# A one-token attention and ReGLU layer: the query product moves from TensorE to VectorE and GpSimd, x is loaded once, and the down products are placed on a block boundary

## The chip, the cores and the metric

The kernel runs on one core of a Trainium2 chip. A core has five engines that run side by side: PE (TensorE, matmuls), DVE (VectorE), ACT (ScalarE), POOL (GpSimd) and SP (SyncE, which here only issues DMA transfers), and 16 DMA engines that move data between the chip's main memory and the core's SBUF. SBUF and PSUM (where matmuls write) both have 128 partitions. The metric is device time in microseconds (us); lower is better. A change of under 0.2% can't be told from none here.

## The reference

One token passes through a pre-norm attention block with a cache of 8192 positions, and then through a gated feed-forward block. All is float32: D = 640, H = 32 heads of Dh = 192, F = 1536.

```python
def _A_ref(x, k_cache, v_cache, wq, wo):
    q = (x @ wq).reshape(B, Sq, H, Dh).transpose(0, 2, 1, 3)
    scores = jnp.einsum("bhqd,bhkd->bhqk", q, k_cache) * (Dh ** -0.5)
    p = _softmax(scores, axis=-1)
    o = jnp.einsum("bhqk,bhkd->bhqd", p, v_cache)
    return o.transpose(0, 2, 1, 3).reshape(B, Sq, H * Dh) @ wo

def _B_ref(x, W_gate, W_up, W_down):
    gate, up = x @ W_gate, x @ W_up
    return (gate * (gate > 0) * up) @ W_down

h = x + _A_ref(_layernorm(x), k_cache, v_cache, wq, wo)
h2 = h + _B_ref(_layernorm(h), W_gate, W_up, W_down)
```

K and V of one head are 6.29 MB each, so the 64 of them make up 403 of the 446 MB that the kernel reads.

## The kernel before, in words

The kernel writes one list of instructions for each engine with the small class `Eng`: `op(fn, after)` appends an instruction and turns each handle in `after` into a semaphore wait, unless that engine has already waited for that value. Each engine runs its list in order. What is written first in the code is first on its engine, and nothing is scheduled afterwards.

There are three large SBUF buffers: `kt[0]` and `kt[1]` (12288 floats in each partition, one head of K each) and `vt` (one head of V). All large transfers are issued by SP, in order, on one DMA queue (q1 in the profile). Each waits only until its buffer is free. At the start the same three buffers hold the query weights `wq`: `wq_t[0]` and `wq_t[1]` lie in `kt[0]`, 2 and 3 in `kt[1]`, and 4 in the first half of `vt`. A row `wq_t[j]` has 6144 floats, the outputs of all heads, for the inputs p*5 + j of the partitions p. So K of head 0 can be loaded when rows 0 and 1 have been used (`h_kfree[0]`), K of head 1 after rows 2 and 3 (`h_kfree[1]`), and V of head 0 after row 4.

Before the loop over heads: x is loaded twice by ACT's queue (`xT`, 128 partitions x 5 floats, and `xrow`, one row of 640). The layer norm makes `xn`, 128 x 5 (PE sums over partitions, by a product with `ones`). PE then forms q with 60 matmuls (L208) in three PSUM banks, ACT copies it out in 12 pieces into `qd` (L216; four partitions hold a quarter of the heads each, all other entries are zero), and PE broadcasts the 192 values of one head to all partitions with the matrix `sel` (L220, and `next_q` at L230 in the loop).

For each head: DVE multiplies K by q (L290, four pieces), POOL folds the halves together (L292), DVE sums the rest (L296) and takes the maximum, and then `kt[h % 2]` is free and SP issues K of head h+2. ACT takes the exponentials (L309), PE multiplies them with V (L240, 32 matmuls), and then `vt` is free and SP issues V of the next head. PE runs its part as a hardware loop (`Fori`). The last entry of `pe.ops.append(("loop", H, body, 32))` is the place, in a block of 256 instructions, where the loop's first instruction is put. The other engines' lists are unrolled.

Behind the loop come the output projection (L342), the layer norm of h, and the up, gate (L379) and down (L393) products, each waiting for its weights, which come on the same queue into buffers as these are freed.

## Time and profile before

| | |
|---|---|
| median of 3 runs | 1041.15 us (1040.79, 1041.15, 1042.88) |
| the profiled execution's own time | 1042.81 us |
| its span, first to last instruction | 1041.2 us |
| busy share of the span | DVE 64%, POOL 43%, PE 35%, PEld 13%, ACT 5% |
| read from main memory | 445.91 MB, 428 GB/s over the span |
| instructions | 6847 |

The profile is of one execution. Its span leaves out 1.6 us of that execution's time. A line of the profile names the engine, the source line, the tile written and the tiles read ("kt<-kt,bank"), how often, and how long; what stands behind `<-` in square brackets is what ended the engine's idle time. "SPq" and "ACTq" are the moments at which SP and ACT issue a DMA. PEclk, or the granted clock, is the share of TensorE's full clock that it was given. A "DMA share" of 1 means that all 16 DMA engines were at work; values a little above 1 come from how packets are split over the windows.

### The profile page before, as it was taken

The numbers are of one execution on the slowest core, as the hardware profiler recorded it, in microseconds if no ns is written. First come the engines' busy times: TensorE is split into PE (matmuls) and PEld (weight loads), VectorE is DVE, ScalarE is ACT, GpSimd is POOL, SyncE is SP. The second block draws the span as 40 slices with busy tenths as digits, with TensorE's granted clock in tenths as the row PEclk, the third lists the DMA queues.
The fourth block names the chain that finished last, engine by engine and source line by source line (L and its number), as shares of the span: only waits on it lengthen the run. The fifth ranks groups of instructions, "written<-read, shape, count | busy, mean of one in ns | idle before, by whom it ended". The sixth has DMA issues, their size and how long they took to land. (4 is left out here: it accounts for less than half of the span.)

```text
span 1041.2 us, 6847 instructions
## 1 busy us (share of the span) xinstructions
PE 361.2 (35%) x2848; PEld 130.8 (13%) x2848; DVE 670.2 (64%) x400; ACT 47.2 (5%) x150; POOL 442.6 (43%) x135
## 2 busy tenths in 40 slices
PE   1504333322333333222233333322133333322385
PEld 0101110111111111001111111101011111101123
DVE  1079677776666667776666667777666666777001
ACT  0201000000000000000000000000000000000010
POOL 2055555554444455555444445555444445555000
PEclk9856665656666666656666666666666666665698
DMA  9999999999999999999999999999999999999997
GB/s 393 446 427 425 444 429 427 444 429 425 446 427 427 442 431 427 440 432 425 442 432 425 442 432 425 442 432 425 442 429 429 442 429 429 440 429 437 420 427 302
DMA packets 11397, 446.05 MB, mean 428 GB/s; under 512 B 1397, under 2 KB 1401, under 8 KB 2042
## 3 DMA queue, kind: packets, MB, share of 16 engines
q1 hardware_dynamic: 11240, 445.91, 99.3%
q8 instruction: 5, 0.08, 0.0%
q14 instruction: 6, 0.05, 0.0%
q10 hardware_dynamic: 146, 0.01, 0.0%
HBM read 445.91 MB, written 0.00 MB: 428 GB/s over the span
## 5 line engine op out<-in xcount | busy, mean ns | idle before, releaser
L292 POOL TENSOR_TENSOR kt<-kt 128x1536 f32<-128x1536 f32 x128 | 436.6, 3443 | 517.5 <-DVE kt L290 517.5
L290 DVE TENSOR_TENSOR kt<-kt,bank 128x3072 f32<-128x3072 f32 x128 | 420.7, 3349 | 143.1 <-DMA kt<-in_A_k_cache_dram 142.6
L240 PE MATMUL bank<-vt,pr 128*2 128x384 f32 x2048 | 238.7, 635 | 546.4 <-PEq L61 546.4
L296 DVE TENSOR_REDUCE sc<-kt 128x16 f32<-128x1536 f32 x128 | 215.2, 1743 | 0.0
L240 PEld LDWEIGHTS bank<-vt,pr 128*2 128x2 f32 x2048 | 57.9, 101 | 706.9 <-issue 706.9
L302 DVE SCALAR_TENSOR_TENSOR oall<-bank,ind,oall 128x193 f32<-128x193 f32 x32 | 13.4, 420 | 137.9 <-PE bank L244 137.9
L311 ACT COPY ob<-bank 128x384 f32<-128x384 f32 x32 | 15.3, 478 | 806.3 <-PE bank L240 806.3
L244 PE MATMUL bank<-ob,par 128*128 128x192 f32 x128 | 28.4, 345 | 22.4 <-PEq L61 22.4
L244 PEld LDWEIGHTS bank<-ob,par 128*128 128x128 f32 x128 | 19.9, 189 | 44.5 <-issue 44.5
L234 PE MATMUL bank<-rs,ones 128*128 128x1 f32 x64 | 14.2, 291 | 27.7 <-PEq L61 27.7
L217 DVE MEMSET bank<- 128x384 f32 x1 | 0.4, 378 | 28.3 <-ACT zt L216 28.3
L227 PE MATMUL bank<-ident,mp 128*1 128x128 f32 x32 | 8.9, 279 | 26.4 <-PEq L61 26.4
L230 PE MATMUL bank<-zt,sel 128*128 x64 | 18.0, 364 | 0.0
L234 PEld LDWEIGHTS bank<-rs,ones 128*128 128x128 f32 x64 | 12.4, 242 | 29.5 <-issue 29.5
L233 PE MATMUL bank<-m,ones 1*128 1x1 f32 x64 | 11.6, 248 | 9.3 <-PEq L61 9.3
L208 PE MATMUL bank<-kt,xn 128*32 128x512 f32 x96 | 13.4, 717 | 4.1 <-DMA kt<-in_A_wq_dram 2.3
L342 PE MATMUL bank<-kt,oT 128*3 128x480 f32 x96 | 11.5, 644 | 1.6 <-DVE oT L333 1.6
L233 PEld LDWEIGHTS bank<-m,ones 1*128 1x128 f32 x64 | 9.8, 190 | 18.2 <-issue 18.2
L367 DVE STREAM_TRANSPOSE hT<-h 128x160 f32<-128x160 f32 x1 | 0.5, 465 | 17.8 <-ACT h L365 17.8
L309 ACT ACTIVATE pr<-sc,nb 128x64 f32<-128x64 f32 x32 | 11.1, 347 | 1.0
L179 DVE TENSOR_REDUCE s<-xT 128x1 f32<-128x5 f32 x1 | 0.2, 158 | 17.0 <-DMA xT<-in_A_x_dram 17.0
L230 PEld LDWEIGHTS bank<-zt,sel 128*128 128x128 f32 x64 | 9.9, 195 | 3.2
(88 smaller groups left out, 104.0 us busy)
## 6 DMA issues: line engine op xcount, KB each, us to landing
kt<-in_A_k_cache_dram SPq DMA_DIRECT2D x32, 6144.0 KB, 35.4
vt<-in_A_v_cache_dram SPq DMA_DIRECT2D x32, 6144.0 KB, 21.6
kt<-in_A_wq_dram SPq DMA_DIRECT2D x2, 6144.0 KB, 24.9
kt<-in_A_wo_dram SPq DMA_DIRECT2D x2, 5760.0 KB, 34.2
vt<-in_A_wo_dram SPq DMA_DIRECT2D x1, 3840.0 KB, 15.5
zt<-in_B_W_up_dram SPq DMA_DIRECT2D x1, 3840.0 KB, 24.3
vt<-in_A_wq_dram SPq DMA_DIRECT2D x1, 3072.0 KB, 40.3
kt<-in_B_W_gate_dram SPq DMA_DIRECT2D x1, 3072.0 KB, 21.6
```

The lines of the kernel that those rows point to most:

```text
L208: a = pe.op(lambda e, j=j, b=b, g=g, c0=c0: e.matmul(qps[b][g * Q:(g + 1) * Q, :], xn[:, j:j + 1].to_broadcast([P, Q]), wq_t[j][:, c0:c0 + ...
L230: return e.matmul(qb, sel, qd[:, bass.ds(i * DH + DH, DH)], start=True, stop=True)
L233: pe.op(lambda e: e.matmul(pb[:, 0:1], ones[0:1, :], m1, start=True, stop=True), takes=[(to_pe["m1"], 1)], sig=pe.sem)
L234: pe.op(lambda e: e.matmul(po2[:, DH:DH + 1], ones, rs, start=True, stop=True), takes=[(to_pe["exp"], 1)])
L240: pe.op(lambda e, i=i, g=g: e.matmul(po[g * Q:g * Q + 2, :], pr[:, 2 * i:2 * i + 2], vt[:, 2 * i * DH:2 * (i + 1) * DH], start=(i < NQ), s ...
L244: pe.op(lambda e, k=k: e.matmul(po2[:, 0:DH], par[:, k, :], ob[:, k * DH:(k + 1) * DH], start=(k == 0), stop=(k == 1)), takes=[(to_pe["ob" ...
L290: a = dve.op(lambda e, ks=ks, h=h: e.tensor_mul(ks, ks, qb[:, None, :].to_broadcast([P, SUB, DH])), [h_k[h], h_qb[h]])
L292: fold.append(pool.op(lambda e, ks=ks: e.tensor_add(ks[:, :, 0:HD], ks[:, :, 0:HD], ks[:, :, HD:DH]), [a]))
L296: a = dve.op(lambda e, ks=ks, i=i, h=h: e.reduce_sum(sc[h % 2][:, i * SUB:(i + 1) * SUB], ks[:, :, 0:HD], axis=AX.X), [fold[i]])
L302: return dve.op(lambda e: e.scalar_tensor_tensor(oall, po2, ind[:, h:h + 1], oall, op0=ALU.mult, op1=ALU.add), [in_loop(h, T_O), (dve.sem, ...
L311: act.op(lambda e: e.copy(ob, po), [in_loop(h, T_V)], sig=to_pe["ob"])
L342: a = pe.op(lambda e, i=i, j=j, g=g: e.matmul(acc3[g * Q:g * Q + 3, :], oT[:, j:j + 3], wo_t[i][:, j - WJ[i]:j - WJ[i] + 3, g * DG:(g + 1) ...
```

## The change

Four things are changed.

1. The query product. `wq_t[j]` is no longer multiplied on PE. DVE takes its first 5120 columns (`QS`) and POOL the other 1024: each multiplies the row by the per-partition scalar `xn[:, j]` and adds it up in `qd`, which now holds a partial sum in every partition. DVE does multiply and add in one instruction (L211), POOL in two (L213, in place in the weights' buffer, and L214). The sum over partitions is left to the product that broadcast the head's q: it uses `ones` where it used `sel` (L219, L229). The 60 matmuls, the 12 copies of ACT and `sel` are gone. `h_q[j]` is now a pair of handles, one of DVE and one of POOL, and the loads of K and V into `kt` and `vt` wait for both.
2. x is loaded once, as a row. `xT` becomes a PSUM tile that PE writes with five transposes of one column each (L178).
3. POOL zeroes only the last 192 columns of `qd`, which `next_q` reads in the last turn of the loop.
4. The loop's head is put at place 88 of its block instead of 32, and `addr_align` in front of the down products makes them start at the beginning of a block of 256 instructions.

```diff
-    hx = load(xT, x[0, 0].rearrange("(p j) -> p j", p=P), "xT", eng=act)
     hxr = load(xrow, x[0], "xrow", eng=act)
...
-    h_qd = pool.op(lambda e: e.memset(qd, 0.0))
+    h_qd = pool.op(lambda e: e.memset(qd[:, H * DH:], 0.0))
...
-    a = dve.op(lambda e: e.reduce_sum(s1, xT, axis=AX.X), [hx])
+    xT, xj = pa[:, 0:DJ], xrow.rearrange("o (p j) -> o j p", j=DJ)
+    for j in range(DJ):
+        a = pe.op(lambda e, j=j: e.transpose(xT[:, j:j + 1], xj[:, j, :], ident[0:1, 0:1]), [hxr, h_id])
+    a = dve.op(lambda e: e.reduce_sum(s1, xT, axis=AX.X), [a])
...
+    QS = 5 * H * DH // 6
     h_q = []
+    d = q = None
     for j in range(DJ):
-        for b in range(NQB):
-            for g in range(NQ):
-                c0 = g * QW + b * QB
-                a = pe.op(lambda e, j=j, b=b, g=g, c0=c0: e.matmul(
-                    qps[b][g * Q:(g + 1) * Q, :], xn[:, j:j + 1].to_broadcast([P, Q]), wq_t[j][:, c0:c0 + QB],
-                    start=(j == 0), stop=(j == DJ - 1)), [h_xn, hwq[j]])
-        h_q.append(a)
-    h_qc = []
...
-    h_po = dve.op(lambda e: e.memset(po, 0.0), [h_qc[-1]])
+        w, x1 = wq_t[j], xn[:, j:j + 1]
+        wd, wp, ad, ap = w[:, 0:QS], w[:, QS:], qd[:, 0:QS], qd[:, QS:H * DH]
+        if j == 0:
+            d = dve.op(lambda e, wd=wd, x1=x1, ad=ad: e.tensor_scalar(ad, wd, x1, None, op0=ALU.mult), [h_xn, hwq[j]])
+            q = pool.op(lambda e, wp=wp, x1=x1, ap=ap: e.tensor_scalar(ap, wp, x1, None, op0=ALU.mult), [h_xn, hwq[j]])
+        else:
+            d = dve.op(lambda e, wd=wd, x1=x1, ad=ad: e.scalar_tensor_tensor(ad, wd, x1, ad, op0=ALU.mult, op1=ALU.add),
+                       [hwq[j], d])
+            t = pool.op(lambda e, wp=wp, x1=x1: e.tensor_scalar(wp, wp, x1, None, op0=ALU.mult), [hwq[j]])
+            q = pool.op(lambda e, wp=wp, ap=ap: e.tensor_add(ap, ap, wp), [t, q])
+        h_q.append([d, q])
+    h_po = dve.op(lambda e: e.memset(po, 0.0))
...
-    h_qb[0] = pe.op(lambda e: e.matmul(qb, sel, qd[:, 0:DH], start=True, stop=True), [h_seln, h_qc[-1]])
+    h_qb[0] = pe.op(lambda e: e.matmul(qb, ones, qd[:, 0:DH], start=True, stop=True), [h_ones] + h_q[-1] + [h_qd])
...
-    pe.ops.append(("loop", H, body, 32))
+    pe.ops.append(("loop", H, body, 88))
...
+    align = lambda e: e.addr_align(256, offset=0, max_nops=0)
+    pe.op(align, sig=False)
     for j in range(FJ):
```

What this does to the order on the engines, at the places that matter. On DVE, between the layer norm and the first product with K, as a piece of the difference (`zt` is the tile in which `qd` lies, `kt` and `vt` hold the weights `wq`):

```order
 L196 COPY fix<-ident 128x128 x3
-L198 TENSOR_REDUCE sel<-ident 128x1
-L199 COPY sel<-sel 128x127
-L200 TENSOR_REDUCE ind<-ident 128x32
-L201 TENSOR_REDUCE ind<-ident 128x4
-L217 MEMSET bank 128x384
+L198 TENSOR_REDUCE ind<-ident 128x32
+L199 TENSOR_REDUCE ind<-ident 128x4
+L208 TENSOR_SCALAR zt<-kt,xn 128x5120
+L211 SCALAR_TENSOR_TENSOR zt<-kt,xn,zt 128x5120 x3
+L211 SCALAR_TENSOR_TENSOR zt<-vt,xn,zt 128x5120
+L216 MEMSET bank 128x384
```

Five instructions of 5120 columns now stand ahead of the first product with K (L290). On POOL, the list of after at the same place, with the semaphores that each waits for:

```order
L163 MEMSET zt 128x192
L209 TENSOR_SCALAR zt<-kt0,xn 128x1024 [waits dma_k0,s_dve]
L213 TENSOR_SCALAR kt0<-kt0,xn 128x1024
L214 TENSOR_TENSOR zt<-zt,kt0 128x1024 [waits s_pool]
L213 TENSOR_SCALAR kt1<-kt1,xn 128x1024 [waits dma_k1]
L214 TENSOR_TENSOR zt<-zt,kt1 128x1024 [waits s_pool]
L213 TENSOR_SCALAR kt1<-kt1,xn 128x1024
L214 TENSOR_TENSOR zt<-zt,kt1 128x1024 [waits s_pool]
L213 TENSOR_SCALAR vt<-vt,xn 128x1024 [waits dma_w4]
L214 TENSOR_TENSOR zt<-zt,vt 128x1024 [waits s_pool]
```

Nine instructions stand where POOL had none; all of them read SBUF while DVE's read SBUF too. On SP, the first rows of before:

```order
L142 DMA kt<-in_A_wq_dram 128x12288
L142 DMA vt<-in_A_wq_dram 128x6144
L142 DMA kt<-in_A_k_cache_dram 128x12288 [waits s_pe] x2
L142 DMA vt<-in_A_v_cache_dram 128x12288 [waits s_pe]
L142 DMA kt<-in_A_k_cache_dram 128x12288 [waits s_dve]
```

and of after:

```order
L140 DMA kt<-in_A_wq_dram 128x12288
L140 DMA vt<-in_A_wq_dram 128x6144
L140 DMA kt<-in_A_k_cache_dram 128x12288 [waits s_pool,s_dve] x2
L140 DMA vt<-in_A_v_cache_dram 128x12288 [waits s_pool,s_dve]
L140 DMA kt<-in_A_k_cache_dram 128x12288 [waits s_dve]
```

The transfers stand in the same order; the first three of the cache wait for POOL and DVE now, where they waited for PE.

## The prediction

> **What bounds the kernel now.** I read the page's slices, the queues and what SP waits for first, then the start and the end in order of time.

> ```profile
> DMA  9999999999999999999999999999999999999997
> DMA packets 11397, 446.05 MB, mean 428 GB/s; under 512 B 1397, under 2 KB 1401, under 8 KB 2042
> q1 hardware_dynamic: 11240, 445.91, 99.3%
> q8 instruction: 5, 0.08, 0.0%
> ...
> q10 hardware_dynamic: 146, 0.01, 0.0%
> ...
> SPq L142 <- PE bank L240: 887.7, 32, 29.3
> SPq L142 <- PE bank L208: 43.8, 3, 28.9
> ...
> kt<-in_A_k_cache_dram SPq DMA_DIRECT2D x32, 6144.0 KB, 35.4
> vt<-in_A_v_cache_dram SPq DMA_DIRECT2D x32, 6144.0 KB, 21.6
> kt<-in_A_wq_dram SPq DMA_DIRECT2D x2, 6144.0 KB, 24.9
> vt<-in_A_wq_dram SPq DMA_DIRECT2D x1, 3072.0 KB, 40.3
> xT<-in_A_x_dram ACTq DMA_DIRECT2D x1, 2.5 KB, 18.0
> ```

> The DMA engines are full in every slice but the last. One transfer of 6.29 MB takes 6.29 / 0.428 = 14.7 us, yet K lands 35.4 us after its issue and V 21.6 us: they stand in the queue for 21 and 7 us. SP's long waits for PE therefore cost nothing as long as an issue comes before the queue runs dry. So the time is: start of the stream + bytes / rate + what follows the last bytes. The change leaves the bytes alone (445.91 MB, less 2.5 KB). It can only move the first three issues of K and V, and the end.

> The start, in order of time:

> ```profile
> 0.74 0.87 SPq L142 DMA_DIRECT2D kt<-in_A_wq_dram  x2
> 18.75 0.16 DVE L179 TENSOR_REDUCE s<-xT 128x1 f32<-128x5 f32 x1 [16.98 <-DMA xT<-in_A_x_dram]
> 22.52 0.23 DVE L188 TENSOR_SCALAR xn<-xc,rstd 128x5 f32<-128x5 f32 x1
> 22.80 8.03 PE L208 MATMUL bank<-kt,xn 128*32 128x512 f32 x48 [1.75 <-DVE par L191]
> 24.24 0.37 DVE L201 TENSOR_REDUCE ind<-ident 128x4 f32<-128x128 f32 x1
> 30.98 7.97 SPq L142 DMA_DIRECT2D kt<-in_A_k_cache_dram  x2
> 33.14 5.36 PE L208 MATMUL bank<-kt,xn 128*32 128x512 f32 x48 [2.30 <-DMA kt<-in_A_wq_dram]
> ...
> 38.63 0.33 SPq L142 DMA_DIRECT2D kt<-in_A_k_cache_dram  x1
> 41.98 4.41 PE L208 MATMUL bank<-vt,xn 128*32 128x512 f32 x24 [3.49 <-DMA vt<-in_A_wq_dram]
> 46.54 0.33 SPq L142 DMA_DIRECT2D vt<-in_A_v_cache_dram  x1
> 52.92 0.98 PE L220 MATMUL bank<-zt,sel 128*128 128x192 f32 x2 [6.53 <-ACT zt L216]
> 56.50 13.15 DVE L290 TENSOR_TENSOR kt<-kt,bank 128x3072 f32<-128x3072 f32 x4 [3.19 <-DMA kt<-in_A_k_cache_dram]
> ...
> 0.00:2.00 2.00, 0.00 (x0) 0.00 (x0) 0.84 (x4) 0.24 (x1) 1.40 (x7) 1.00 0.75 221
> 2.00:4.00 2.00, 0.00 (x0) 0.00 (x0) 0.00 (x0) 1.04 (x1) 2.00 (x1) 1.00 0.56 172
> ```

> The weights land at about 18.6 us (the mean of two is 24.9, and the second came 31.9 after its issue at 1.2), 33.1 and 42.0. K of head 0 was issued at 30.98, K of head 1 at 38.63, V at 46.54, and q was ready at 53.9, still 2.6 us before K landed at 56.50.

> **When the queue runs dry.** In the first 4 us 0.79 MB moved, which at 428 GB/s is 1.8 us of work. From an issue into an empty queue (0.74) the stream thus loses 4.0 - 0.74 - 1.8 = 1.4 us. Query weights (15.73 MB) and K of head 0 (6.29 MB) take 51.4 us from an effective start at 2.2, to 53.6. An issue of K of head 1 up to 53.6 - 1.4 = 52.2 us costs nothing. Each us later is lost for good, since nothing behind it has spare time on a full queue. The limits of the others are softer: K of head 0 by 2.2 + 15.73 / 0.428 - 1.4 = 37.5, V 14.7 us after K of head 1's limit.

> **The change, part by part.**

> ```profile
> L292 POOL TENSOR_TENSOR kt<-kt 128x1536 f32<-128x1536 f32 x128 | 436.6, 3443 | 517.5 <-DVE kt L290 517.5
> L290 DVE TENSOR_TENSOR kt<-kt,bank 128x3072 f32<-128x3072 f32 x128 | 420.7, 3349 | 143.1 <-DMA kt<-in_A_k_cache_dram 142.6
> L166 POOL MEMSET zt<- 128x6336 f32 x1 | 5.4, 5377 | 0.0
> ...
> L292 POOL TENSOR_TENSOR kt<-kt x128: 3428/3440/3474, 59.9 to 957.3; 128x1536 f32<-128x1536 f32 x128
> L290 DVE TENSOR_TENSOR kt<-kt,bank x128: 3344/3348/3356, 56.5 to 953.4; 128x3072 f32<-128x3072 f32 x128
> ...
> 62.00:64.00 2.00, 0.00 (x0) 0.00 (x0) 2.00 (x2) 0.00 (x0) 2.00 (x2) 0.50 0.91 393
> ```

> 1. *x as one row.* `xT` was 128 pieces of 20 bytes, 8 for each DMA engine, taking turns with weight rows of 48 KB at 428/16 = 26.8 GB/s, 1.84 us each: 8 turns and one for the semaphore make 16.6 us, about the 18.0 shown. One row has one piece: two turns, so I take it to land near 7 us. The lower bound is about 2, the upper 22 (the old 18.0 and two turns more). Five transposes can't cost more than five times L220's 0.98 us; I take 1.5, since they are of one column and not of 192. The norm takes 4.0 us as before (18.75 to 22.75) and the small DVE work behind it 1.9 (22.7 to 24.6). DVE is ready at 7 + 1.5 + 4.0 + 1.9 = 14.4, before the weights at 18.6. With both upper bounds it is ready at 32.8, and K of head 0 is issued at 44.0, 6.5 us after its limit; I give that no chance of its own, because two turns would have to last like eleven. The stream itself gains the 128 small packets: 146 packets of q10 show 0.0%, so 0.1 us at most.

> 2. *DVE's share.* By L290's 1.09 ns per column, 5120 columns take 5.6 us, 28 us in all. Rows 0 and 1: 18.6 to 29.8, so K of head 0 is issued at 29.8, against 30.98. Rows 2 and 3: 33.1 to 44.3, and K of head 1 is issued at 44.3, against 38.63: later, but 7.9 us before the limit. Row 4: to 49.9, and V at 49.9, against 46.54, inside its limit.

> 3. *POOL's share.* The addition by L292's 2.24 ns per column: 2.3 us for 1024. The scaling has one input and is bounded by L166's 0.85 (0.9 us) and L292's 2.24 (2.3 us); I take 1.0, near the memset. That is 1.0 for row 0 and 3.3 for each other, less than DVE's 5.6, so it is hidden behind DVE if both run side by side, as L290 and L292 do in the window of 62 to 64 us.

> 4. *q and the first head.* PE forms q after 49.9, about 1.0 us (L220), and no copy of ACT follows: 50.9 against 53.9. K lands at 56.5 either way, so the earlier q gains nothing and DVE has 5.6 us of cover. PE has no work in which the 60 matmuls' absence could show.

> 5. *Removed:* 60 matmuls, 12 copies, `sel`: all beside the stream, nothing. The shorter memset: nothing, since POOL is idle there until 18.6.

> 6. *The end.* The weights of the down product land last:

> ```profile
> 1026.02 3.43 PE L379 MATMUL bank<-kt,hT 128*32 128x384 f32 x40 [2.52 <-DMA kt<-in_B_W_gate_dram]
> 1032.62 6.37 PE L393 MATMUL bank<-kt,guT 128*32 128x160 f32 x96 [3.17 <-DMA kt<-in_B_W_down_dram]
> ...
> 1028.00:1030.00 2.00, 1.45 (x20) 0.37 (x12) 0.41 (x1) 0.00 (x0) 0.00 (x0) 1.00 0.96 407
> 1032.00:1034.00 2.00, 1.38 (x24) 1.20 (x28) 0.00 (x0) 0.00 (x0) 0.00 (x0) 0.50 0.86 337
> 1034.00:1036.00 2.00, 2.00 (x36) 1.70 (x32) 0.00 (x0) 0.00 (x0) 0.00 (x0) 0.50 0.23 92
> 1036.00:1038.00 2.00, 2.00 (x39) 1.66 (x35) 0.00 (x0) 0.00 (x0) 0.00 (x0) 0.50 0.05 17
> ...
> 1032.48 0.14 issue
> 1032.62 6.49 PE bank L393 x96
> ```

> L393 runs without a gap from the landing of its first weights: 96 records in 6.49 us. A start on a block boundary can take no stall away, for there is none. What holds it is the clock of 0.50. L379 does 40 records of 384 columns in 3.43 us at 1.00, so 96 of 160 columns would take 3.43 x (96 x 160) / (40 x 384) = 3.4 us; then the last bytes (about 1037) would bound, and the end would come some 2 us sooner. That is the distance of the runs, 1040.79 and 1042.88, and the profiled execution (1042.81) is of the slower sort. I read it as the phase of the clock's changes, which the edit doesn't touch. Skipping to the boundary costs at most a fetch of instructions. PE is through L379 at 1029.45 and its next weights come at 1032.48, so 3 us of it are covered.

> [...]

> **Sum.** Against the profiled execution's own 1042.8: -0.1 for the small packets, 0 for all else, 1042.7 with the slow clock at the end and about 1040.9 with the other. The median of the runs, 1041.15, is of the second sort. I forecast 1041.2.

> **The rivals.**

> *DVE and POOL shut each other out (slower).* L290 has one input in SBUF and one in PSUM, and L296 one in all. They overlap with POOL freely. The new DVE instructions have two SBUF inputs (`kt`, `zt`), and no row shows such a one beside POOL, so it may be that they take turns, an instruction at a time. The bounds: free (44.3 as above), or wholly in turn. In turn, rows 2 to 4 begin at 33.1. Before K of head 1 stand DVE's rows 2, 3 and, because row 4 has landed at 42.0 and each engine slips in when the other ends, row 4 too: 3 x 5.6 + 2 x 3.3 = 23.4, so the issue comes at 56.5. That is 4.3 us past 52.2: about 1045.4. With the scaling at 2.3 us it would be 6.9 us, 1048.1. If POOL were let through before DVE's row 4, it would be 17.8 us, issue at 50.9, and nothing lost. It decides from 52.2 us on. For it: the cover is only 7.9 us and the turns would need 12.2. Against it: nothing in this trace shows such a turn. The two engines' other pairs cost each other nothing: L290 varies from 3344 to 3356 ns, its first run without POOL included, and L292 from 3428 to 3474.

> [...]

> *The end is lifted (faster).* In the windows from 1034 to 1038 a share of 0.23 and 0.05 of the DMA engines is still at work: a few engines finish some 3 us behind the others. If these lag because of code that PE fetched during the stream, then 60 fewer matmuls take some of it away: up to 3 us, 1038. Against it: queue q8, which carries code, shows 5 packets and 0.08 MB in all, and which engine lags for what I can't tell.

> *The jump stalls PE (slower).* A fetch of over 3 us in the full queue would show at the end: 1042 to 1043.

> **How the numbers follow.** Forecast 0.50; turns of DVE and POOL 0.38; lifted end 0.08; jump 0.04. The forecast alone is 1040.6 to 1042.9. With the turns' 1045.4, and 1046.2 for part of the dearer scaling, the range is 1039.8 to 1046.2; it leaves out most of the lifted end and the turns' upper bound. A measurement of this kernel can't tell 0.2% (2.1 us) from no change: below 1039.07 is faster, above 1043.23 slower. Faster 0.08, same 0.52 (the forecast and half of the jump), slower 0.40.

> **What would show it.** Right: x lands near 7 us; DVE's L208 and L211 take 5.6 us and POOL's L213/L214 1.0 and 2.3 while both run; K of head 1 is issued near 44 us, the DMA share shows no hole between 52 and 60 us; L290 starts at 56.5. Wrong: L211 or L214 stretched to the length of the other engine's instruction, SP waiting for POOL until 56 us, a hole of some 4 us in the DMA share, and all that follows later by it.

## The result: 1046.78 us, 0.54% slower, and the profile after

The changed kernel takes 1046.78 us (median of 5 runs, 1046.48 to 1047.96), beside 1041.15 for the kernel before (by now five runs, 1040.79 to 1042.88). The ratio is 1.0054, 95% interval 1.004 to 1.0069. The profiled execution took 1046.48 us, with a span of 1045.0. The forecast of 1041.2 and its range up to 1046.2 were wrong. What happened is the rival "DVE and POOL shut each other out", with a larger price than it was given.

First the start of the changed kernel in order of time. The columns are start, length, engine and line, tiles, how many; in brackets stands the idle time before. L208 and L211 are DVE's share of the five rows, L209, L213 and L214 are POOL's.

```profile
2.06 0.73 PE L178 MATMUL bank<-ident,xrow 1*128 1x1 f32 x5 [2.06 <-DMA xrow<-in_A_x_dram]
18.55 2.89 DVE L208 TENSOR_SCALAR zt<-kt,xn 128x5120 f32<-128x5120 f32 x1 [10.19 <-DMA kt<-in_A_wq_dram]
18.70 5.44 POOL L209 TENSOR_SCALAR zt<-kt,xn 128x1024 f32<-128x1024 f32 x1 [17.21 <-DMA kt<-in_A_wq_dram]
32.98 25.03 SPq L140 DMA_DIRECT2D kt<-in_A_k_cache_dram  x2
33.05 11.87 DVE L211 SCALAR_TENSOR_TENSOR zt<-kt,xn,zt 128x5120 f32<-128x5120 f32 x2 [5.30 <-DMA kt<-in_A_wq_dram]
33.12 8.20 POOL L213 TENSOR_SCALAR kt<-kt,xn 128x1024 f32<-128x1024 f32 x1 [0.24 <-DMA kt<-in_A_wq_dram]
41.40 5.73 POOL L214 TENSOR_TENSOR zt<-zt,kt 128x1024 f32<-128x1024 f32 x1
45.03 7.44 DVE L211 SCALAR_TENSOR_TENSOR zt<-vt,xn,zt 128x5120 f32<-128x5120 f32 x1
47.11 8.07 POOL L213 TENSOR_SCALAR kt<-kt,xn 128x1024 f32<-128x1024 f32 x1
55.27 2.34 POOL L214 TENSOR_TENSOR zt<-zt,kt 128x1024 f32<-128x1024 f32 x1
57.58 2.84 POOL L213 TENSOR_SCALAR vt<-vt,xn 128x1024 f32<-128x1024 f32 x1
```

The same four DVE instructions one by one, in the view of source line L211 (least, median and longest in ns, then the first and last start):

```profile
L211 DVE SCALAR_TENSOR_TENSOR zt<-kt,xn,zt x3: 5552/6284/6286, 21.5 to 38.6; 128x5120 f32<-128x5120 f32 x3
L211 DVE SCALAR_TENSOR_TENSOR zt<-vt,xn,zt x1: 7441/7441/7441, 45.0 to 45.0; 128x5120 f32<-128x5120 f32 x1
```

Read POOL first. Alone, from 55.27 on, its addition takes 2.34 us and its scaling 2.84. Beside DVE they take 5.73, and 8.20 and 8.07. Now see where the long ones end. DVE's row 2 runs from 33.05 for 5.55 us, to 38.60, and row 3 for 6.29 us, to 44.92. POOL's scaling, begun at 33.12, ends at 41.32, which is 2.7 us after row 2. The addition, begun at 41.40, ends at 47.13, 2.2 us after row 3. The scaling begun at 47.11 ends at 55.18, 2.7 us after row 4. Each POOL instruction got next to nothing done until the DVE instruction beside it was over, and then took its own length.

DVE is held too, but by less. Row 2, first to start, takes 5.55 us. Row 3 takes 6.29, 0.73 more; beside it begins POOL's scaling, which has one tile as input. Row 4 takes 7.44, 1.89 more, beside an addition of two tiles. So in the chain from 33.05 to the issue of K of head 1, the terms are three DVE instructions of 5.55 (16.7), 0.73 and 1.89 by which DVE was held, then the rest of the scaling (2.7) and the addition (2.34), and some 0.3 of small gaps. They add up to 24.6 us. The two issues that L140 lists from 32.98 span 25.03 us; the second came 0.33 before their end, at 57.68.

What SP waited for, in the waits of its queue (us in total, times, longest), and the shares in windows of 4 us (PE, PEld, DVE, ACT and POOL busy, then granted clock, DMA share, GB/s):

```profile
SPq L63 <- POOL zt L214: 60.0, 3, 30.8
```

```profile
52.00:56.00 4.00, 0.00 (x0) 0.00 (x0) 0.85 (x2) 0.00 (x0) 3.92 (x2) 1.00 0.09 37
56.00:60.00 4.00, 0.00 (x0) 0.00 (x0) 0.00 (x0) 0.00 (x0) 4.00 (x2) 1.00 0.66 197
60.00:64.00 4.00, 0.98 (x2) 0.50 (x2) 0.00 (x0) 0.00 (x0) 2.76 (x2) 1.00 0.86 369
```

The three issues that the change moves all waited for POOL's L214. From 52 to 56 us the DMA engines stand at a share of 0.09; DVE is done by 52.9 and only POOL is at work. That hole is the loss, and nothing makes it up behind it. In the page's slices it is the one digit that differs from before, and at the end the down product starts later:

```profile
DMA  9989999999999999999999999999999999999997
```

```profile
1037.64 5.24 PE bank L395 x96
```

This line is from the chain that ended last. In the profile before, an execution of 1042.81 us, the down product began at 1032.62; here it is 5.0 us later.

### The profile page after: what moved, and what is told of

It reads as the page before. It is cut to its first block, busy times and chain, and to the rows that moved or that the text cites. A ratio compares the mean times of both kernels' runs of the same rounds, so it can differ in the third digit from the quotient of the medians.

```text
span 1045.0 us, 6621 instructions
## 1 busy us (share of the span) xinstructions
PE 342.9 (33%) x2733; PEld 127.0 (12%) x2733; DVE 698.4 (67%) x403; ACT 41.0 (4%) x138; POOL 481.0 (46%) x144
## 3 DMA queue, kind: packets, MB, share of 16 engines
q1 hardware_dynamic: 11240, 445.91, 99.0%
HBM read 445.91 MB, written 0.00 MB: 427 GB/s over the span
## 5 line engine op out<-in xcount | busy, mean ns | idle before, releaser
L292 POOL TENSOR_TENSOR kt<-kt 128x1536 f32<-128x1536 f32 x128 | 436.5, 3444 | 466.9 <-DVE kt L290 466.9
L290 DVE TENSOR_TENSOR kt<-kt,bank 128x3072 f32<-128x3072 f32 x128 | 420.7, 3349 | 149.3 <-DMA kt<-in_A_k_cache_dram 137.0
L296 DVE TENSOR_REDUCE sc<-kt 128x16 f32<-128x1536 f32 x128 | 215.2, 1744 | 0.0
L243 PEld LDWEIGHTS bank<-ob,par 128*128 128x128 f32 x128 | 19.9, 189 | 44.5 <-issue 44.5
L213 POOL TENSOR_SCALAR kt<-kt,xn 128x1024 f32<-128x1024 f32 x3 | 22.6, 7536 | 0.2 <-DMA kt<-in_A_wq_dram 0.2
L211 DVE SCALAR_TENSOR_TENSOR zt<-kt,xn,zt 128x5120 f32<-128x5120 f32 x3 | 18.1, 6041 | 5.4 <-DMA kt<-in_A_wq_dram 5.3
L219 PE MATMUL bank<-zt,ones 128*128 128x192 f32 x2 | 1.0, 593 | 57.9 <-POOL zt L214 57.9
L229 PE MATMUL bank<-zt,ones 128*128 x64 | 17.8, 361 | 0.0
L209 POOL TENSOR_SCALAR zt<-kt,xn 128x1024 f32<-128x1024 f32 x1 | 5.4, 5444 | 17.2 <-DMA kt<-in_A_wq_dram 17.2
L308 ACT ACTIVATE nb<-bank 128x1 f32<-128x1 f32 x32 | 5.5, 171 | 154.2 <-PE bank L232 154.2
## 6 DMA issues: line engine op xcount, KB each, us to landing
kt<-in_A_k_cache_dram SPq DMA_DIRECT2D x32, 6144.0 KB, 35.5
vt<-in_A_v_cache_dram SPq DMA_DIRECT2D x32, 6144.0 KB, 21.4
kt<-in_A_wq_dram SPq DMA_DIRECT2D x2, 6144.0 KB, 24.8
vt<-in_A_wq_dram SPq DMA_DIRECT2D x1, 3072.0 KB, 38.7
kt<-in_B_W_gate_dram SPq DMA_DIRECT2D x1, 3072.0 KB, 20.6
```

The source lines that it names most:

```text
L211: d = dve.op(lambda e, wd=wd, x1=x1, ad=ad: e.scalar_tensor_tensor(ad, wd, x1, ad, op0=ALU.mult, op1=ALU.add), [hwq[j], d])
L213: t = pool.op(lambda e, wp=wp, x1=x1: e.tensor_scalar(wp, wp, x1, None, op0=ALU.mult), [hwq[j]])
L229: return e.matmul(qb, ones, qd[:, bass.ds(i * DH + DH, DH)], start=True, stop=True)
L243: pe.op(lambda e, k=k: e.matmul(po2[:, 0:DH], par[:, k, :], ob[:, k * DH:(k + 1) * DH], start=(k == 0), stop=(k == 1)), takes=[(to_pe["ob" ...
L290: a = dve.op(lambda e, ks=ks, h=h: e.tensor_mul(ks, ks, qb[:, None, :].to_broadcast([P, SUB, DH])), [h_k[h], h_qb[h]])
L292: fold.append(pool.op(lambda e, ks=ks: e.tensor_add(ks[:, :, 0:HD], ks[:, :, 0:HD], ks[:, :, HD:DH]), [a]))
```

## The experiments

The theory after the result: DVE's row products (two SBUF inputs) and POOL's instructions that read SBUF shut each other out, so POOL is late, so SP issues K of head 1 after the queue has run dry, and the time is the hole. The rivals: POOL's instructions are merely slow; the late q, not the hole, costs the time; the edits of x or of the placement cost it. All medians below stand beside runs of the kernel before on the same chip with medians of 1041.07 to 1041.13.

**DVE does all five rows.** Every other part of the change stays.

```diff
-    QS = 5 * H * DH // 6
+    QS = H * DH
...
-            q = pool.op(lambda e, wp=wp, x1=x1, ap=ap: e.tensor_scalar(ap, wp, x1, None, op0=ALU.mult), [h_xn, hwq[j]])
...
-            t = pool.op(lambda e, wp=wp, x1=x1: e.tensor_scalar(wp, wp, x1, None, op0=ALU.mult), [hwq[j]])
-            q = pool.op(lambda e, wp=wp, ap=ap: e.tensor_add(ap, ap, wp), [t, q])
-        h_q.append([d, q])
+        h_q.append([d])
```

> DVE takes all 6144 columns of each row, POOL none; all else as in the changed kernel. Theory (POOL's share is shut out while DVE runs, so K of head 1 is issued at 57.7 us, 5.5 us after the queue's limit of 52.2): with no POOL share, rows 2 and 3 take two instructions of some 6.55 us (5.55 us for 5120 columns, times 1.2 less the fixed part) from 33.05, K of head 1 is issued at 46.3, no hole in the DMA share between 52 and 64 us, and the time is that of before, 1041 (1040.3 to 1042.9). Rival (the loss lies in the end, in the jump to the block boundary or in the loop's new place, or in the single row of x): all of these are still there, so the time stays at 1046 to 1048.

Measured: 1041.02 us (11 runs, 1040.65 to 1042.41), ratio 1.0000, interval 0.9991 to 1.0009. The start in order of time, and the windows:

```profile
28.60 18.05 SPq L140 DMA_DIRECT2D kt<-in_A_k_cache_dram  x2
33.02 13.27 DVE L210 SCALAR_TENSOR_TENSOR zt<-kt,xn,zt 128x6144 f32<-128x6144 f32 x2 [4.44 <-DMA kt<-in_A_wq_dram]
...
1032.04 1.84 PE L392 MATMUL bank<-kt,guT 128*32 128x160 f32 x48 [3.15 <-DMA kt<-in_B_W_down_dram]
```

```profile
52.00:56.00 4.00, 1.01 (x2) 0.50 (x2) 2.53 (x3) 0.00 (x0) 0.00 (x0) 1.00 0.94 406
56.00:60.00 4.00, 0.00 (x0) 0.00 (x0) 4.00 (x2) 0.00 (x0) 1.71 (x1) 1.00 0.96 410
60.00:64.00 4.00, 0.00 (x0) 0.00 (x0) 4.00 (x2) 0.00 (x0) 4.00 (x2) 1.00 0.94 406
```

DVE alone, with a fifth more columns in each instruction, is through row 3 at 46.3 us, and K of head 1 is issued 11.4 us sooner than with POOL's help. The hole is gone and so is the whole loss. From 52 to 64 us this kernel moved (406 + 410 + 406) x 4 = 4.89 MB and the changed one (37 + 197 + 369) x 4 = 2.41 MB; the 2.48 MB between are 5.8 us at 428 GB/s. The down product starts at 1032.04 here and at 1037.64 in the changed kernel, 5.60 us apart. The medians of the changed kernel and of before are 5.6 us apart.

**One SBUF input for DVE.** POOL's work is the changed kernel's; DVE's second input changes, from the running sum in SBUF to a PSUM bank of zeros, 512 columns read over and over. The kernel thus leaves out adding up the rows.

```diff
+    z1 = banks[1]
+    dve.op(lambda e: e.memset(z1, 0.0))
...
-            d = dve.op(lambda e, wd=wd, x1=x1, ad=ad: e.scalar_tensor_tensor(ad, wd, x1, ad, op0=ALU.mult, op1=ALU.add),
-                       [hwq[j], d])
+            d = dve.op(lambda e, wd=wd, x1=x1, ad=ad: e.scalar_tensor_tensor(
+                ad.rearrange("p (a b) -> p a b", b=QB), wd.rearrange("p (a b) -> p a b", b=QB), x1,
+                z1[:, None, :].to_broadcast([P, QS // QB, QB]), op0=ALU.mult, op1=ALU.add), [hwq[j], d])
```

> DVE's second input in rows 1 to 4 is a bank of zeros in PSUM in place of the running sum in SBUF, so rows are not added up on DVE: this part of the computation is left out. Number, size and order of the instructions are the same. Theory (POOL waits because DVE reads two tensors of SBUF): POOL's scaling takes 2.7 to 2.8 us and its addition 2.3 from the landing on, DVE's instruction 5.5 to 5.6; only row 0, where DVE has one input, may still show a turn (the 2.9 us of DVE's row 0 point to a mode of its own). K of head 1 is issued at about 44.2 to 44.5 and the time is that of before, 1041 (1040.3 to 1042.9). Rival (POOL's scaling is slow in itself, 5 to 8 us each): POOL's instructions keep 5.4 to 8.2 us, K of head 1 is issued after 52, and the time is 1044 to 1047.

Measured: 1040.95 us (11 runs, 1040.68 to 1041.43), ratio 0.9998, interval 0.9989 to 1.0007. In order of time (here DVE's rows are L210 and L213, POOL's L211, L216 and L217):

```profile
18.74 2.89 DVE L210 TENSOR_SCALAR zt<-kt,xn 128x5120 f32<-128x5120 f32 x1 [10.37 <-DMA kt<-in_A_wq_dram]
18.90 5.44 POOL L211 TENSOR_SCALAR zt<-kt,xn 128x1024 f32<-128x1024 f32 x1 [17.41 <-DMA kt<-in_A_wq_dram]
29.67 15.06 SPq L140 DMA_DIRECT2D kt<-in_A_k_cache_dram  x2
33.24 11.13 DVE L213 SCALAR_TENSOR_TENSOR zt<-kt,xn,bank 128x5120 f32<-128x5120 f32 x2 [6.03 <-DMA kt<-in_A_wq_dram]
33.31 2.84 POOL L216 TENSOR_SCALAR kt<-kt,xn 128x1024 f32<-128x1024 f32 x1 [3.73 <-DMA kt<-in_A_wq_dram]
36.23 2.35 POOL L217 TENSOR_TENSOR zt<-zt,kt 128x1024 f32<-128x1024 f32 x1
```

Two DVE rows now take 11.13 us together, 5.55 each, and POOL's pair takes 2.84 and 2.35 beside them, as it does alone. POOL was not slow, and it is not the mere company of DVE: it is DVE's second input from SBUF. K of head 1 is issued at 29.67 + 15.06 - 0.33 = 44.4 us, where step 2 of the prediction had it, and the time is that of before. Only row 0 still shows a turn (POOL 5.44 us), to which the next experiment comes.

**POOL only writes.** Its nine instructions become memsets of the same 1024 columns, so POOL's share of q is left out; DVE's stay as in the changed kernel.

```diff
-            q = pool.op(lambda e, wp=wp, x1=x1, ap=ap: e.tensor_scalar(ap, wp, x1, None, op0=ALU.mult), [h_xn, hwq[j]])
+            q = pool.op(lambda e, ap=ap: e.memset(ap, 0.0), [h_xn, hwq[j]])
...
-            t = pool.op(lambda e, wp=wp, x1=x1: e.tensor_scalar(wp, wp, x1, None, op0=ALU.mult), [hwq[j]])
-            q = pool.op(lambda e, wp=wp, ap=ap: e.tensor_add(ap, ap, wp), [t, q])
+            t = pool.op(lambda e, wp=wp: e.memset(wp, 0.0), [hwq[j]])
+            q = pool.op(lambda e, ap=ap: e.memset(ap, 0.0), [t, q])
```

> POOL's nine instructions are memsets of the same 1024 columns, so they write SBUF and read nothing; POOL's sixth of q is left out. DVE is as in the changed kernel. Theory (what the engines take turns for is the reading): POOL's memsets take about 0.9 us each and are not held up by DVE's instructions of rows 1 to 4, DVE's take 5.55, K of head 1 is issued at 44.3 and the time is 1041 to 1043. Rival (any POOL instruction that touches SBUF waits for DVE's with two inputs): the memsets that start beside one last until its end, 5 us or so, and K of head 1 waits for POOL until after 50.

Measured, a single run: 1041.16 us.

```profile
18.76 3.72 DVE L208 TENSOR_SCALAR zt<-kt,xn 128x5120 f32<-128x5120 f32 x1 [10.39 <-DMA kt<-in_A_wq_dram]
18.85 0.95 POOL L209 MEMSET zt<- 128x1024 f32 x1 [17.34 <-DMA kt<-in_A_wq_dram]
19.74 3.63 POOL L213 MEMSET kt<- 128x1024 f32 x1
...
33.28 11.14 DVE L211 SCALAR_TENSOR_TENSOR zt<-kt,xn,zt 128x5120 f32<-128x5120 f32 x2 [5.21 <-DMA kt<-in_A_wq_dram]
33.30 0.95 POOL L213 MEMSET kt<- 128x1024 f32 x1 [8.93 <-DMA kt<-in_A_wq_dram]
```

Beside DVE's two-input rows the memsets take 0.95 us and DVE its 5.55: no turn. So the turns beside L211 took both: two DVE inputs in SBUF (8.20 us for POOL's scaling, 2.84 with one of them in PSUM) and a read by POOL (0.95 us for a memset). Row 0 is another matter. DVE's L208, with one input and a scalar, does 5120 columns in 2.89 us, about twice as fast as L211, and there even writing contends. L208 takes 3.72 us in this run. The first memset, begun 0.09 us after it, still takes its own 0.95 us, and DVE is held for about as long (0.83); the second waits and takes 3.63 us, ending at 23.37, 0.9 us after L208's end at 22.48.

Which of the two began second did not settle who waited. POOL's instructions that read, second to begin beside L211 in the changed kernel, got next to nothing done until it was over. DVE's rows 3 and 4, second there, were held only 0.73 and 1.89 us by instructions of 2.84 and 2.34, and the first memset, second to begin beside L208, was not held.

**Row 4 behind POOL.** The rival of the prediction said that if POOL were let through before DVE's row 4, nothing would be lost.

```diff
             d = dve.op(lambda e, wd=wd, x1=x1, ad=ad: e.scalar_tensor_tensor(ad, wd, x1, ad, op0=ALU.mult, op1=ALU.add),
-                       [hwq[j], d])
+                       [hwq[j], d] + ([h_q[3][1]] if j == 4 else []))
```

> DVE's instruction for row 4 waits for POOL's row 3; all work is as in the changed kernel. Theory (the late issue is due to DVE's row 4 standing between POOL's instructions): DVE's row 3 ends at 44.9, POOL's addition for row 2 at 47.1, its row 3 takes 2.8 + 2.3 us more, and K of head 1 is issued at 52.3, at the limit: time within 0.7 us of before, 1040.8 to 1042.9, though q is as late as in the changed kernel (64 us) and the first product with K begins there. Rival (the late q, that is the first product with K at 64.1 instead of 56.5, sets the time): the time stays at 1046 to 1048.

Measured: 1042.28 us (11 runs, 1041.61 to 1043.71), ratio 1.0012, interval 1.0003 to 1.0021.

```profile
32.92 19.81 SPq L140 DMA_DIRECT2D kt<-in_A_k_cache_dram  x2
47.07 2.84 POOL L213 TENSOR_SCALAR kt<-kt,xn 128x1024 f32<-128x1024 f32 x1
49.99 2.34 POOL L214 TENSOR_TENSOR zt<-zt,kt 128x1024 f32<-128x1024 f32 x1
52.46 6.30 DVE L211 SCALAR_TENSOR_TENSOR zt<-vt,xn,zt 128x5120 f32<-128x5120 f32 x1 [7.58 <-POOL zt L214]
61.11 0.98 PE L219 MATMUL bank<-zt,ones 128*128 128x192 f32 x2 [55.98 <-POOL zt L214]
```

One wait more, on DVE, wins back 4.5 of the 5.6 us, because the issue moves from 57.68 to 52.40. DVE's row 4 ends later (58.8), and q comes only at 62.1. Where the 1.15 us that are left come from is taken up behind the next series.

**A late issue alone.** DVE does all rows, and K of head 1 waits for copies of ACT that nothing else needs: eight, three and five of them.

```diff
+        if j == 3:
+            for i in range(NLATE):
+                d3 = act.op(lambda e: e.copy(late, ones[:, None, :].to_broadcast([P, 12, P])), [d, h_ones] + ([d3] if i else []))
+            h_late = d3
...
-    h_kfree = [h_q[1], h_q[3]] + [None] * H
+    h_kfree = [h_q[1], [h_late]] + [None] * H
```

> As with DVE alone, but K of head 1 waits for eight copies of ACT (128 x 1536, about 1.5 us each, doing nothing else) that begin when DVE has done row 3. POOL has no share, q is ready at about 54 us and the first product with K begins when K of head 0 lands (55 us). Theory (the time lost is the hole in the queue, and each us of the issue after 52.2 us is lost for good): K of head 1 is issued at 46.3 + 11.8 = 58.1, 0.4 us later than in the changed kernel, the DMA share shows the same hole, and the time is 1046.5 to 1048.5. Rival (the loss comes from the late q and the late first product): here both are early, and the time is 1041 to 1042.9.

> DVE alone, K of head 1 behind three copies of ACT in place of eight: issued at 46.4 + 4.5 = 50.9 us. Theory (nothing is lost up to about 52.2, and each us beyond it in full): the time is that of before, 1040.7 to 1041.6 in most runs. Rival (the price rises with every us of lateness, since 12 us late cost 6.4): half of the lateness, about 2.4 us slower.

> The same behind five copies: issued at 46.4 + 7.5 = 53.9 us. Theory with the limit of 52.2: 1.7 us slower than before, 1042.8; with the limit that the run with eight copies gives (58.5 less 6.4 = 52.1) 1.8; with that of the run in which row 4 stands behind POOL (52.4 less 1.2 = 51.2) 2.7. So 1042.7 to 1043.9.

Measured with eight: 1047.57 us (5 runs, 1047.2 to 1048.71), ratio 1.0064, interval 1.0051 to 1.0078. With three: 1041.75 (11 runs, 1041.1 to 1042.29), 1.0003, 0.9994 to 1.0012. With five: 1043.14 (11 runs, 1042.76 to 1043.61), 1.0016, 1.0007 to 1.0026. The start with eight copies, in order of time, and the first window of the hole:

```profile
28.76 30.07 SPq L140 DMA_DIRECT2D kt<-in_A_k_cache_dram  x2
46.48 11.99 ACT L216 COPY late<-ones 128x1536 f32<-128x1536 f32 x8 [40.82 <-DVE zt L211]
53.23 1.01 PE L221 MATMUL bank<-zt,ones 128*128 128x192 f32 x2 [48.09 <-DVE zt L211]
55.01 13.15 DVE L292 TENSOR_TENSOR kt<-kt,bank 128x3072 f32<-128x3072 f32 x4 [1.38 <-DMA kt<-in_A_k_cache_dram]
```

```profile
52.00:56.00 4.00, 1.01 (x2) 0.50 (x2) 2.54 (x3) 3.91 (x4) 0.00 (x0) 1.00 0.13 53
```

The issue of K of head 1, first with five copies, then with three (the same window is in the table below):

```profile
54.18 0.33 SPq L140 DMA_DIRECT2D kt<-in_A_k_cache_dram  x1
```

```profile
50.78 0.33 SPq L140 DMA_DIRECT2D kt<-in_A_k_cache_dram  x1
```

With eight copies q is there at 54.2, 0.3 us later than in the kernel before, and the first product with K begins at 55.01, 1.5 us sooner, and still the time is lost. So it takes no late q to lose this time; the hole is enough. The whole series, by the moment at which K of head 1 is issued, with the median above that of the kernel before and what the prediction's limit of 52.2 us gives:

| kernel | issue, us | GB/s in 52 to 56 | measured | issue - 52.2 |
|---|---|---|---|---|
| DVE does all rows | 46.32 | 406 | -0.1 | 0 |
| three copies | 50.78 | 332 | +0.6 | 0 |
| row 4 behind POOL | 52.40 | 295 | +1.15 | 0.2 |
| five copies | 54.18 | 225 | +2.0 | 2.0 |
| the changed kernel | 57.68 | 37 | +5.6 | 5.5 |
| eight copies | 58.50 | 53 | +6.4 | 6.3 |

From 54 us on the limit gives the loss to within 0.15 us, closer than the intervals of about 1 us can vouch for. Issues and GB/s are each read from one profiled execution, and the seven windows of 4 us from 36 to 64 us range from 393 to 504 GB/s in the kernel before, so that column only ranks the holes. Whether the edge at 52.2 us is sharp stays open: the 0.6 us of three copies is within its interval's reach of nothing.

Row 4 behind POOL does not belong to this edge. Its runs fall into two groups, seven from 1041.61 to 1042.40 us and four from 1043.25 to 1043.71, and the profiled one (1043.26) is of the upper group. There a second hole stands behind the first. First its next issue and two longer windows, then the same windows with DVE on all rows:

```profile
82.01 0.33 SPq L140 DMA_DIRECT2D kt<-in_A_k_cache_dram  x1
```

```profile
52.00:80.00 28.00, 0.98 (x2) 0.50 (x2) 24.48 (x9) 0.00 (x0) 22.51 (x7) 1.00 1.00 422
80.00:100.00 20.00, 11.10 (x75) 4.06 (x75) 18.84 (x10) 2.37 (x5) 12.91 (x4) 0.97 0.95 393
```

```profile
52.00:80.00 28.00, 3.23 (x9) 2.08 (x9) 25.37 (x14) 1.90 (x4) 13.88 (x5) 1.00 0.99 425
80.00:100.00 20.00, 10.52 (x75) 4.02 (x75) 17.98 (x11) 1.09 (x4) 13.44 (x4) 0.89 1.00 433
```

From 52 to 80 us 3 GB/s are missing, 0.08 MB or 0.2 us, as the limit says for an issue at 52.40. From 80 to 100 us 40 GB/s are missing, 0.8 MB or 1.9 us. K of head 2 waits for the work of head 0, and that for q; it was issued at 82.01, where the prediction's working would put its limit at 52.2 + 2 x 14.7 = 81.6. So the late q did cost time in this execution, by the same mechanism one transfer further on; why 0.4 us of lateness cost 1.9 is not shown. In the changed kernel K of head 2 was issued later still, at 83.89, but there the late K of head 1 had moved that limit to about 87, and its 80 to 100 us show the full 433 GB/s.

**x as a row alone, and the placement alone**, each added to the kernel before: of the change's diff the lines on `xT` and `xrow`, and the two lines on 88 and `addr_align`.

> The kernel before with one part of the change: x comes as one row and PE transposes it; q stays on PE. The prediction's price for this part was -0.1 us at most. Theory (x is hidden behind the weights either way): xn is ready near 7 us instead of 22.7, PE begins L208 when the weights land (18.6) and K of head 0 is issued at about 27, but the queue is full until 53 us in both, so the time is that of before, 1040.6 to 1042.9. Rival (the small packets of xT or the late x cost the stream something): 0.5 to 2 us faster.

> The kernel before with one part of the change: loop head at place 88 and the down products on a block boundary. The prediction's price was 0. Theory (no stall to take away, and a fetch is covered by the 3 us between gate and down products): the time is that of before, 1040.6 to 1042.9. Rival (the jump to the boundary makes PE fetch, or the new place delays a DMA engine near the end): 1 to 3 us slower.

Measured: x as a row 1041.01 us (11 runs, 1040.79 to 1042.56), ratio 1.0001, interval 0.9992 to 1.001. The placement 1041.16 us (11 runs, 1040.9 to 1042.32), 1.0001, 0.9992 to 1.001. With x as a row, in order of time:

```profile
6.61 0.23 DVE L190 TENSOR_SCALAR xn<-xc,rstd 128x5 f32<-128x5 f32 x1
25.60 16.07 SPq L142 DMA_DIRECT2D kt<-in_A_k_cache_dram  x2
```

The norm is ready 16 us sooner and K of head 0 is issued 5.4 us sooner, at 25.60. Neither gains anything: in the kernel before, too, the queue is full all that time (9 in each slice of its page but the last).

**PE kept busy ahead of the down product.** DVE does all rows, and three products of which nothing is used stand between the gate and the down products. There the granted clock went from 1.00 (1028 to 1030 us) to 0.50 (1032 to 1038 us) in the profile before.

```diff
+    for _ in range(3):
+        pe.op(lambda e: e.matmul(banks[6], ident, up_t[:, 0, 0:512], start=True, stop=True))
     align = lambda e: e.addr_align(256, offset=0, max_nops=0)
```

> DVE alone, as in the first experiment, with three products of 512 columns into a free bank (their result is not used) between the gate and the down products, about 2.6 us at full clock, to fill PE's pause. Theory (the slower of the two sorts of runs, 1042.4 beside 1041.0, is a down product at half clock, because PE paused before it): the down products run at 1.0 in every execution and none of the runs is above 1041.6; the median is 1040.8 to 1041.1, so this would be the fastest version by some tenths. Rival (the two sorts come from elsewhere, such as the order of the last landings): runs of 1042 to 1043 still occur, 1 in 5 or so.

Measured: 1041.11 us (11 runs, 1040.71 to 1041.34), ratio 1.0000, interval 0.9991 to 1.0009. The median is not lower, and none of the 11 runs lies near 1042.4. That proves little. Without the products 2 of 11 lay there, on another chip; on this chip it was 1 of 27 of the kernel before, and 1 of 11 each with x as a row and with the placement. Whether the three products prevent the slower sort stays open.

The kept profiles say more about what that sort is. The run with three copies took 1042.29 in its profiled execution, the highest of its 11:

```profile
1032.39 6.32 PE L397 MATMUL bank<-kt,guT 128*32 128x160 f32 x96 [3.16 <-DMA kt<-in_B_W_down_dram]
```

The 96 products last 6.32 us there without a gap. In the profile before (1042.81) they last 6.37 us, at a granted clock of 0.50 from 1032 to 1038 us. In the six profiled executions of 1040.86 to 1041.28 us the down product was through in 5.0 to 5.2 us; with DVE on all rows 48 of the products last 1.84, and then they wait for weights. In the changed kernel's profile it took 5.14 us, at 0.57 and 0.58 in the two windows from 1038 to 1042 us and 1.00 in those before and behind them. So a half clock through the whole down product goes with some 1.2 us more. No version that was run beats the kernel before beyond the noise.

## Why the prediction was wrong

- **The limit and its price: right.** "Each us later is lost for good" and 52.2 us fit the medians to 0.15 us from 54 on (the table). Below that the runs leave the shape of the edge open. What the working lacked is the limit of K of head 2, 81.6 us, which a late q can miss.
- **Step 1, x as one row: right in effect, wrong in size.** x landed at 2.06 us, not near 7, at the lower bound; the two turns behind weight rows were not needed. Such turns were the author's estimate, set against the 18.0 us of `xT`; no view shows them. The landing of x lies under the cover of the weights' landing at 18.55, and alone it is worth nothing (1.0001).
- **Step 2, DVE's share: right where DVE runs free.** 5.55 us instead of 5.6 for rows 1 to 4, and issue at 44.4 with one SBUF input. Row 0 was mis-sized: 2.89 us, since the operation with one input and a scalar ran about twice as fast as L290 suggested (0.56 ns per column against 1.09).
- **Step 3, POOL's share: the step that failed.** The sum put POOL's 3.3 us for each row at nothing: "so it is hidden behind DVE if both run side by side, as L290 and L292 do in the window of 62 to 64 us". L290 has one input in SBUF and one in PSUM. The new rows have two in SBUF, so the pair taken as evidence was of another kind than the pair to be judged. The rival said this itself, and yet the free case was made the likeliest on the ground that no row showed a turn; no row of that trace held such a pair, so its silence said nothing. What came in its place: POOL waited out DVE's rows (8.20 us for 2.84 of work), and K of head 1 was issued at 57.68 us and not at 44.3. The experiment with one SBUF input shows that DVE's second input decides this, since the issue came at 44.4 there.
- **The scaling's price: mis-sized.** 2.84 us, where 1.0 was taken between 0.9 and 2.3. It lies above both bounds: here POOL took longer to multiply by a scalar from another tile than to add two tiles. The addition was right (2.34 for 2.3).
- **The rival's working: right mechanism, short by 1.2 us in the issue.** It gave 56.5 and 1045.4; 57.68 and 1046.8 came. Three DVE instructions stood in the way as it said, row 4 among them. Its 6.6 us for two scalings and two additions became 0.73 + 1.89 + 2.7 + 2.34 = 7.7, and gaps of 0.3. That it came so near is partly luck, since two mistakes in its terms cancel in part: the two scalings are dearer by 3.7 us, but of the scaling and the addition that held DVE, 5.2 us in length, only 2.6 came on the path. That leaves 1.1 us. With its own variant, the scaling at 2.3, it would have had 1048.1. Its remark that POOL let through before row 4 loses nothing was off by 1.15 us at the median: the issue came at 52.40 and not 50.9, and the remark left out that a q this late holds up K of head 2.
- **Steps 4 and 5: right.** An early q gains nothing (the eight copies), and the matmuls and copies taken away cost and gained nothing (DVE on all rows: 1.0000).
- **Step 6, the end: right.** The placement alone costs and gains nothing (1.0001). Of the rivals of the end, neither the lifted end nor the jump shows in any median. That a half clock in the down product goes with the upper level fits the profile before (6.37 us at 0.50, 1042.81) beside the changed kernel's 5.14 us at a higher clock; that it is the phase of the clock's changes is not shown.

## What to carry to other kernels

Before two engines are set side by side on one job, look where each operand lies: here a DVE instruction with two inputs in SBUF and a POOL instruction that reads SBUF got in each other's way, POOL waiting for the whole of DVE's (8.20 us for 2.84 of work), and instructions of the same size with DVE's second input in PSUM ran at once (2.84 us beside 5.55). Trust only a row of the profile with the same operand places as evidence that two engines overlap; where there is none, the turn-taking belongs in the sum, with its full chain up to the next DMA issue. For a kernel bound by its transfers, work out the moment at which the queue runs dry and compare each issue with it, the later ones that hang on the same result too, keeping a us or two in hand.
